# Loading w1 of a decode kernel by two transfers from two queues, with x behind the first

## The chip, the core and the metric

The kernel runs on one core of one Trainium2 chip. A core has TensorE (PE, with its weight loads shown apart as PEld), VectorE (DVE), ScalarE (ACT), GpSimd (POOL) and SyncE (SP); 16 DMA engines move data between the chip's main memory and the core's on-chip memory of 128 partitions. SyncE and ScalarE can both issue transfers, each on a queue of its own. The metric is the time of one execution in microseconds; shorter is better.

## What is computed

One decode step (one token for each of 4 batch rows, D = 576) of a block with two branches that share a layer norm of x: attention over the last 2048 positions of a cache of 16 KV heads with 32 query heads of 128, and a mixer followed by an MLP.

```python
x  = A_x                                   # [4, 1, 576]
xn = layernorm(x)
# branch A
q = xn @ wq                                # 32 heads of 128
k, v = the last 2048 rows of the caches    # 16 heads, each used by 2 query heads
A = softmax(q k^T / sqrt(128)) v @ wo
# branch B, on layernorm(xn)
h  = gelu(layernorm(xn) @ w1)              # 576 x 576
hs = shift(h) @ w2                         # shifts along the sequence, which has length 1
x1 = xn + hs
B  = x1 + gelu(layernorm(x1) @ w3) @ w4    # 576 x 4608, 4608 x 576
return x + A + B
```

With a sequence of length 1 every shift moves its rows out and zeros in, so the product with w2 is one with zeros.

## The kernel before, in words

Every engine's instructions are written out by hand: `add(engine, ..., key=...)` appends one with the events that it waits for and a sort key, and at the end each engine's list is sorted by key. `add_dma` does so for a transfer; each transfer counts on a semaphore of its own name, and the returned event is the full count of what has been issued under that name so far. Without `engine=` it goes to SyncE's list.

SyncE's list holds all the large transfers. By their keys: w1 (-50), w2 (-49), wq (-48), w3 (-47), then the 16 chunks of K (2 MB each, key 0 to 15), the 8 chunks of V (4 MB each, the last in two pieces), w4 and the five pieces of wo. The first four and the first two K chunks wait for nothing. K chunk 2 waits for the last matmul that reads wq (event "q"), as wq lies in the buffer of K's slots 2 and 3; from chunk 4 on, each waits until chunk c - 4 has been transposed. V and the last weights wait for buffers in the same way. A matrix of 576 rows is laid out by `runs`: 9 half rows lie one after the other on each of 128 partitions, so w1 and w2 are 128 rows of 5184 bytes each.

ScalarE's list begins with the transfer of x (4 rows of 1152 bytes, key -100) and ends with that of the output.

The work at the start, in order: VectorE takes the statistics of x (L305, L306, L308), ScalarE the square root (L310), VectorE normalises (L312, L314, L318), and does the same once more on xn for branch B. TensorE transposes both (L330), VectorE spreads them into `xs` (L336). TensorE then goes through its list in this order: the product with w1 (L397, nine matmuls, waits for w1 and xs), the two halves of the product with w2 (L405), the transposes of the third layer norm (L330), the product with wq (L369, 36 matmuls), transposes of q (L380), the zeroing of two PSUM banks (L360), and the product with w3 (L430), which waits for w3. After that comes the long part: for each K chunk 64 transposes (L485), copies out of PSUM on VectorE and ScalarE (L469, L468) and 16 score matmuls (L492); softmax; the products with V (L553); and the products with w4 and wo (L392), whose sum is copied to the output (L608, L609).

`t1`, the sum of x and x1 (L414), reads x once more and is used near the end.

Of the kernel before, what the change touches and what calls it, by code (L numbers as in the profile page):

```python
# [37 lines left out]
def bass_parallel_sum__sliding_block_cached__mixer_s_mlp__decode_kernel(  # L38
# [27 lines left out]
    x2 = A_x.rearrange("b s d -> (b s) d")  # L66
# [3 lines left out]
    with ExitStack() as ctx:  # L70
        def sb(name, shape, dt):
            return ctx.enter_context(nc.sbuf_tensor(name, shape, dt))

        def sem(name):
            return ctx.enter_context(nc.semaphore(name))
# [22 lines left out]
        def cut(n):  # L98
            nonlocal _o
            _o += n  # L100
            return ktb[:, _o - n:_o]
        w1_t = cut(9 * HALF)
# [10 lines left out]
        x_sb = sb("x_sb", [B, D], BF16)  # L113
# [74 lines left out]
        def add(engine, emit, waits=(), sig=None, key=0.0, inc=None):  # L188
            seqc[0] += 1
            prog[engine].append(Op(emit, waits, sig, key, seqc[0], inc))  # L190

        def add_dma(pairs, skey, waits=(), key=0.0, engine="sp"):
            if skey not in S:
                S[skey] = sem("s_" + "_".join(str(k) for k in (skey if isinstance(skey, tuple) else (skey,))))
            dma_count[skey] = dma_count.get(skey, 0) + 16 * len(pairs)

            def emit(e):
                for o_, i_ in pairs:
                    e.dma_start(o_, i_).then_inc(S[skey], 16)  # L199
            add(engine, emit, waits, None, key)  # L200
            return ("dma", skey, dma_count[skey])

        def runs(w_ap):
            return w_ap.rearrange("(m e) n -> m (e n)", e=9).rearrange("m (a x) -> (m a) x", a=2)
# [60 lines left out]
        add("dve", lambda e: e.tensor_copy(out=mH_bf[:], in_=mH[:].unsqueeze(2).to_broadcast([128, NX, 2])), waits=["mH"], sig="mH_bf", key=-7.8)  # L265


        ev_x = add_dma([(x_sb[:], x2)], "x", (), -100, engine="act")
        ev_wq = add_dma([(wq_t, runs(A_wq))], "wq", (), -48)
        ev_w1 = add_dma([(w1_t, runs(B_w1))], "w1", (), -50)  # L270
        ev_w2 = add_dma([(w2_t, runs(B_w2))], "w2", (), -49)
        ev_w3 = add_dma([(w3_t, runs(B_w3))], "w3", (), -47)
        ev_w4 = add_dma([(w4_t, B_w4.rearrange("(p r) n -> p r n", r=W4R))], "w4", [f"PV{2 * (NCV - NVS + 1) + 1}"], KS + NCV)
# [444 lines left out]
```

## Time and profile before

| | |
|---|---|
| median of 3 runs | 213.94 us (213.77 to 214.14) |
| the profiled execution | 213.93 us |
| its span in the profile | 212.6 us |
| PE / PEld busy | 172.5 us (81%) / 133.7 us (63%) |
| DVE / ACT / POOL busy | 111.9 us / 58.6 us / 15.6 us |
| DMA | 88.65 MB in 5066 packets, mean 417 GB/s |

The span is the stretch that the profiler records; the time of the execution is a little longer. In the lists of the trace, a row gives the source line (L199 is the line in `add_dma` that issues a transfer), the engine, the operation, the tiles written and read, and the count. "SPq" and "ACTq" are the instruction queues of SyncE and ScalarE, which issue transfers and count as busy with nothing else. In brackets stands how long the engine was idle before and what released it. "To landing" is the time from a transfer's issue to its completion. In a table of windows the columns are the stretch, its length, busy time (and instructions) of PE, PEld, DVE, ACT and POOL, the clock granted to TensorE, the mean busy share of the 16 DMA engines, and GB/s.

### The profile page before, as it was taken

To read this page: it belongs to the slowest core of one execution; us is meant where nothing else is said; L and a number is where in the kernel's file an instruction comes from. 1 tells how busy PE (TensorE), PEld (TensorE's weight loads), DVE (VectorE), ACT (ScalarE), POOL (GpSimd) and SP (SyncE) were. 2 spreads that over 40 slices of the span, in tenths; PEclk is the share of its full clock that TensorE was granted. 3 is DMA by queue.
4 is the path that set the end of the run, shared out by engine and by line. 5 is a ranking of instruction groups with operands and counts; after the bars stand their busy time and mean duration, and the time that the engine had idled before them with its cause. 6 is when DMAs were issued, how large, how long until landed. Compare 5 with 4: busy or idle time off the path is not lost.

```text
span 212.6 us, 4856 instructions
## 1 busy us (share of the span) xinstructions
PE 172.5 (81%) x2212; PEld 133.7 (63%) x2216; DVE 111.9 (53%) x168; ACT 58.6 (28%) x69; POOL 15.6 (7%) x38
## 2 busy tenths in 40 slices
PE   1456147999999999999996089999989598997495
PEld 0222014888878888887774048988868487883262
DVE  5433200477776777777764869995575444003000
ACT  2004001366665566666656520000000000000000
POOL 8991000000000000000000000000000000000000
PEclk9997855899999999999999589999999889999799
DMA  6999999999999999999999999999999999999993
GB/s 242 453 444 445 429 396 416 432 425 427 429 416 438 432 422 429 435 422 424 432 444 438 444 407 459 413 425 453 407 444 438 419 425 410 451 476 393 407 408 131
DMA packets 5066, 88.65 MB, mean 417 GB/s; under 512 B 568, under 2 KB 704, under 8 KB 1216
## 3 DMA queue, kind: packets, MB, share of 16 engines
q1 hardware_dynamic: 5040, 88.49, 97.7%
q8 instruction: 8, 0.13, 0.3%
q14 instruction: 2, 0.02, 0.0%
q10 hardware_dynamic: 16, 0.01, 0.0%
HBM read 88.49 MB, written 0.00 MB: 416 GB/s over the span
## 4 chain that ended last, share of the span: by engine, by line
DMA 47%; PE 45%; DVE 4%; SPq 1%; ACT 1%; issue 1%
PE ps L485 23%; DMA vring<-in_A_wo_dram 15%; DMA vring<-in_B_w_dram 13%; DMA vring<-in_A_v_cache_dram 12%; PE ps L553 11%; DMA kring<-in_A_k_cache_dram 7%; PE ps L492 6%; PE ps L430 2%; SPq L199 1%; DVE vring L520 1%; DVE rmax L498 1%; DVE ktb L545 1%; PE ps L514 1%; PE ps L347 1%; ACT ktb L468 0%
## 5 line engine op out<-in xcount | busy, mean ns | idle before, releaser
L469 DVE COPY ktb<-ps 128x1024 bf16<-128x1024 bf16 x80 | 53.8, 689 | 23.5 <-PE ps L485 23.4
L485 PEld LDWEIGHTS ps<-perm_bf,kring 128*128 128x128 bf16 x1024 | 58.2, 98 | 8.3 <-issue 7.6
L485 PE MATMUL ps<-perm_bf,kring 128*128 128x128 bf16 x1024 | 61.7, 220 | 0.2
L468 ACT ACTIVATE ktb<-ps 128x1024 bf16<-128x1024 bf16 x48 | 48.0, 1023 | 32.5 <-PE ps L485 32.1
L545 DVE TENSOR_TENSOR ktb<-kring,mH_bf 128x4096 bf16<-128x4096 bf16 x16 | 36.2, 2286 | 14.6 <-PE ps L553 14.6
L553 PE MATMUL ps<-vring,ktb 128*128 128x256 bf16 x256 | 30.3, 282 | 4.3 <-DMA vring<-in_A_v_cache_dram 3.5
L553 PEld LDWEIGHTS ps<-vring,ktb 128*128 128x128 bf16 x256 | 25.7, 101 | 8.5 <-issue 3.6
L553 PE MATMUL ps<-kring,ktb 128*128 128x256 bf16 x256 | 28.6, 273 | 0.9 <-DMA kring<-in_A_v_cache_dram 0.9
L553 PEld LDWEIGHTS ps<-kring,ktb 128*128 128x128 bf16 x256 | 25.0, 98 | 4.5 <-issue 1.1
L608 ACT ACTIVATE out_sb<-ps 4x288 bf16<-4x288 f32 x1 | 0.4, 399 | 84.6 <-PE ps L392 84.6
L492 PE MATMUL ps<-ktb,Qs 128*32 128x512 bf16 x272 | 17.8, 382 | 1.2 <-ACT ktb L468 1.2
L430 PE MATMUL ps<-vring,xs 128*8 128x320 bf16 (+1 forms) x72 | 4.5, 429 | 7.6 <-DMA vring<-in_B_w_dram 7.6
L492 PEld LDWEIGHTS ps<-ktb,Qs 128*32 128x32 bf16 x272 | 5.7, 96 | 6.7 <-DVE ktb L469 1.4
L514 PE MATMUL ps<-vring,pick_bf 128*32 128x256 bf16 x64 | 3.9, 411 | 6.4 <-DVE rinv L532 6.4
L609 DVE CAST out_sb<-ps 4x288 bf16<-4x288 f32 x1 | 0.4, 449 | 15.7 <-PE ps L392 15.7
L392 PE MATMUL ps<-vring,h2T_sb 128*4 128x288 bf16 x72 | 6.2, 347 | 3.1 <-DMA vring<-in_B_w_dram 3.1
L571 DVE TENSOR_SCALAR tmp<-ps,maskd 128x128 f32<-128x128 f32 x2 | 0.7, 350 | 14.8 <-PE ps L553 14.8
L430 PEld LDWEIGHTS ps<-vring,xs 128*8 128x8 bf16 x72 | 2.1, 110 | 9.8 <-DMA vring<-in_B_w_dram 8.0
L330 PE MATMUL ps<-ident_bf,xp_bf 4*128 4x4 bf16 x15 | 0.8, 163 | 8.1 <-DVE xp_bf L314 5.0
L392 PEld LDWEIGHTS ps<-vring,h2T_sb 128*4 128x4 bf16 x72 | 3.7, 101 | 5.8 <-DMA vring<-in_B_w_dram 3.6
L514 PEld LDWEIGHTS ps<-vring,pick_bf 128*32 128x32 bf16 x64 | 2.0, 118 | 8.2 <-DVE rinv L532 6.9
L239 POOL MEMSET ktb<- 128x8192 bf16 x1 | 6.9, 6924 | 0.0
(93 smaller groups left out, 78.6 us busy)
## 6 DMA issues: line engine op xcount, KB each, us to landing
kring<-in_A_k_cache_dram SPq DMA_DIRECT2D x16, 2048.0 KB, 13.8
vring<-in_A_v_cache_dram SPq DMA_DIRECT2D x4, 4096.0 KB, 24.6
kring<-in_A_v_cache_dram SPq DMA_DIRECT2D x3, 4096.0 KB, 34.0
vring<-in_B_w_dram SPq DMA_DIRECT2D x2, 5184.0 KB, 25.1
kring<-in_A_wq_dram SPq DMA_DIRECT2D x1, 4608.0 KB, 15.7
kring<-in_A_v_cache_dram SPq DMA_DIRECT2D x2, 2048.0 KB, 27.4
vring<-in_A_wo_dram SPq DMA_DIRECT2D x1, 1872.0 KB, 26.9
vring<-in_A_wo_dram SPq DMA_DIRECT2D x1, 1440.0 KB, 29.8
```

The source lines that it names most:

```text
L199: e.dma_start(o_, i_).then_inc(S[skey], 16)
L239: P(lambda e: e.memset(ktb[:, NKT // 2 * 1024:NKT * 1024], 0.0), key=-92, inc=(("E", LB - 2), 1))
L347: ins = e.matmul(ps[:, w, :], lhsT=zeros_bf[:, 0:128], rhs=zeros_bf[:, :], start=True, stop=True)
L392: return e.matmul(ACC[h], lhsT=lhsT, rhs=rhs, start=start, stop=stop, tile_position=(0, 32 * h), skip_group_check=True)
L430: ins = e.matmul(H2ps[k][32 * j:32 * j + 2 * B].rearrange("b (p t) -> b p t", t=n), lhsT=x_at(2, s_), rhs=w[:, :, 9 * j + t0:9 * j + t0 + ...
L468: return "act", lambda e: e.activation(out=ktbuf[:, n % NKT], in_=tb[n % 4], func=ACTF.Copy)
L469: return "dve", lambda e: e.tensor_copy(out=ktbuf[:, n % NKT], in_=tb[n % 4])
L485: ins = e.transpose(tb[j % 4][:, t, :], kslot_t(k)[:, 8 * kb + t, :], perm_bf[:])
L492: ins = e.matmul(Sps[32 * u:32 * u + 32, q, :].rearrange("p (t i) -> p t i", t=16), lhsT=Qs[:, k, 32 * u:32 * u + 32], rhs=ktgrp[:, (4 * k ...
L514: ins = e.matmul(ps[32 * j:32 * j + 32, 4 + qt, 256 * ih:256 * (ih + 1)].rearrange("p (t a e) -> p t a e", a=NPAIR, e=2), lhsT=pick_bf[:, ...
L545: return lambda e: e.tensor_tensor(out=PTpad[:, n % 4], in0=PTv[:, qt, NH * h:NH * (h + 1), bp, :].unsqueeze(2).to_broadcast([128, NH, NX, ...
L553: ins = e.matmul(ps[:, 0, 0:256], lhsT=PTpad[:, 2 * (k % 2) + h, 2 * g:2 * g + 2].rearrange("p t h e -> p (t h e)"), rhs=vslot(k)[:, Dh * ...
```

## The change

w1's single transfer from SyncE becomes two: the odd partitions are issued by ScalarE as the first entry of its list, in the place of x, and the even partitions by SyncE as the first entry of its list. Both count on the same semaphore, and the product with w1 waits for the full count of both. x is issued by SyncE with the key -49.5, that is between the even half of w1 and w2. Nothing else is changed.

```diff
-        ev_x = add_dma([(x_sb[:], x2)], "x", (), -100, engine="act")
+        ev_x = add_dma([(x_sb[:], x2)], "x", (), -49.5)
         ev_wq = add_dma([(wq_t, runs(A_wq))], "wq", (), -48)
-        ev_w1 = add_dma([(w1_t, runs(B_w1))], "w1", (), -50)
+        add_dma([(w1_t[1:128:2], runs(B_w1)[1:128:2])], "w1", (), -100, engine="act")
+        ev_w1 = add_dma([(w1_t[0:128:2], runs(B_w1)[0:128:2])], "w1", (), -50)
         ev_w2 = add_dma([(w2_t, runs(B_w2))], "w2", (), -49)
```

## The prediction

> **What bounds the kernel now.** I read the page's head first, then the DMA rate by stage, then the chain that ended last, then the first 30 us instruction by instruction.
>
> From the page: the span, the 40 slices of the span with the share and the rate of the DMA engines, and the one queue (SyncE's) that carries nearly all bytes.
>
> ```profile
> span 212.6 us, 4856 instructions
> ...
> DMA  6999999999999999999999999999999999999993
> GB/s 242 453 444 445 429 396 416 432 425 427 429 416 438 432 422 429 435 422 424 432 444 438 444 407 459 413 425 453 407 444 438 419 425 410 451 476 393 407 408 131
> ...
> q1 hardware_dynamic: 5040, 88.49, 97.7%
> q10 hardware_dynamic: 16, 0.01, 0.0%
> ```
>
> Only the first and the last slice are not full. The same by stages (the last two columns are the DMA share and GB/s):
>
> ```profile
> 0.00:2.50 2.50, 0.61 (x1) 0.10 (x1) 0.26 (x1) 1.10 (x1) 1.84 (x8) 1.00 0.26 60
> 2.50:30.00 27.50, 10.31 (x92) 4.99 (x96) 10.18 (x34) 3.07 (x7) 13.80 (x31) 0.85 1.01 429
> 30.00:110.00 80.00, 78.52 (x1309) 63.54 (x1303) 52.24 (x93) 45.58 (x47) 0.00 (x0) 0.94 1.01 430
> 110.00:176.00 66.00, 54.05 (x538) 44.59 (x537) 44.77 (x35) 8.47 (x15) 0.00 (x0) 0.92 1.00 428
> 176.00:208.50 32.50, 27.41 (x268) 19.82 (x268) 3.97 (x6) 0.00 (x0) 0.00 (x0) 0.95 1.00 424
> ```
>
> From 2.5 to 208.5 us the 16 DMA engines are full, at 424 to 430 GB/s, whatever the compute does. The kernel is a stream of 88.5 MB with a lead-in and a tail. The tail is short; from the chain that ended last (start, length, what):
>
> ```profile
> 2.17 27.46 DMA vring<-in_B_w_dram
> ...
> 178.35 31.68 DMA vring<-in_A_wo_dram
> 210.03 0.04 issue
> 210.07 0.70 PE ps L392 x8
> 210.78 0.44 DVE out_sb L609
> ```
>
> The last piece of wo is issued 31.68 us before it lands, so the queue is deep even at the end, and after that landing little more than 2 us follow. So the end moves by what the stream as a whole moves, one for one: it can start earlier or later, have a gap, or run at another rate. A delay of an engine counts only if it empties the queue, or if it outlasts the slack before a landing.
>
> **The change part by part.** The start of the timeline (start, length, engine, line, what, count, and in brackets the idle time before it and who ended it):
>
> ```profile
> 0.80 0.85 SPq L199 DMA_DIRECT2D ktb<-in_B_w_dram  x2
> 0.81 0.56 ACTq L199 DMA_DIRECT2D x_sb<-in_A_x_dram  x1
> ...
> 1.40 1.28 ACT L310 ACT_TABLE_LOAD   x1 [1.40 <-PEq L703]
> ...
> 2.17 0.52 SPq L199 DMA_DIRECT2D vring<-in_B_w_dram  x1
> 2.24 0.45 DVE L305 BATCH_NORM_STATS2 stats<-x_sb 4x6 f32<-4x288 bf16 x1 [2.24 <-DMA x_sb<-in_A_x_dram]
> ...
> 2.73 18.97 SPq L199 DMA_DIRECT2D kring<-in_A_k_cache_dram  x4
> ...
> 8.46 2.32 PE L397 MATMUL ps<-ktb,xs 128*8 128x288 bf16 x9 [0.78 <-DVE xs L336]
> ...
> 17.41 3.06 PE L369 MATMUL ps<-kring,xs 128*8 128x512 bf16 x36
> ...
> 21.57 0.54 PE L360 MATMUL ps<-zeros_bf 128*128 128x320 bf16 x2
> ...
> 29.68 2.57 PE L430 MATMUL ps<-vring,xs 128*8 128x320 bf16 x36 [7.56 <-DMA vring<-in_B_w_dram]
> ```
>
> And three answers on single transfers: the spread of the landing times of the B weights (w1 is the shortest, w3 the longest), the same for K, and one wait of SyncE's queue.
>
> ```profile
> DMA to landing us min/median/max: 3.6/13.9/27.5
> ```
> ```profile
> DMA to landing us min/median/max: 12.1/13.8/37.0
> ```
> ```profile
> SPq L199 <- PE ps L369: 16.5, 1, 16.5
> ```
>
> 1. *w1's two halves.* The bytes stay: two times 324 KB for one time 648 KB. I take it that all sixteen engines share each half; no row shows a transfer of 64 rows, and were each half on fewer engines, w2's bytes would fill the others. One transfer more has one more completion, which no row prices and which moves nothing. w1 lands 3.6 us after its issue, at 4.4 us. Its reader, the nine matmuls of L397, starts at 8.46 us, and what releases it is xs from VectorE, not w1. So w1 is 4 us early already. An earlier w1 is worth nothing by itself: its halves matter only through the stream's start.
>
> 2. *x.* It leaves ScalarE's queue, where nothing was ahead of it, and goes behind the even half on SyncE's. Bounds of its delay: at least its issue comes later by the issue of the half ahead (the two issues of w1 and w2 take 0.85 us together, so about 0.4 us each), that is +0.4 us; at most it lands with w1 as it lands today, at 4.4 instead of about 2.2 us, +2.2 us. The engines that carry x must first finish the even rows of their ring, with the odd rows coming in between, so I take +2.0 us. The whole layer norm chain behind x moves with it: L305 to L336 on VectorE and ScalarE, then PE in its order: L397, both L405, L369 (the q matmuls), the transposes, the zeroing of L360. That chain ends at 21.57 + 0.54 = 22.1 us and PE is then idle for 7.56 us, until w3 lands. So it ends at 24.1 us, with 5.6 us to spare. **Cost 0**; what hides it is the wait of L430 for w3, and the delay would have to exceed 7.56 us to show there. What is added in time by a lower TensorE clock if the q matmuls fall elsewhere is bounded by their own 3.06 us again, which still leaves 2.5 us.
>
> 3. *Who waits on that chain besides PE.* SyncE holds back K chunk 2 until the last q matmul (the wait of 16.5 us); it would be issued 2.0 us later, at about 22.5 us. The longest landing of a K transfer is 37.0 us; it belongs to one of the first two chunks, issued from 2.73 us on, so the queue has bytes until about 40 us. The issue comes 17 us before it is needed: **cost 0**, and the cover would be gone only at a delay of 17 us.
>
> 4. *SyncE's own issues.* x is one issue more on its queue (again about 0.4 us), the even half saves at most half of its 0.4 us. So w2 is issued between 0.2 and 0.6 us later than at 1.24, by 1.85 us at the latest, and wq, w3 and the first two K chunks move by as much. w2's bytes are wanted when w1's are through, by 4.4 us at the latest and not before 3.3 us (w1's 664 KB at the full rate take 1.55 us, from 1.7 us on). That w2's data follow its issue by 0.9 us (as w1's do: issue 0.80, first bytes at 1.7) gives 2.75 us. There is 0.5 us of cover at the worst: **cost 0**. ScalarE issues the odd half in place of x, 0.56 us today for four rows; its table load at 1.40 us could slip by the same, and is wanted only by the first Sqrt, after x.
>
> 5. *The stream's start, the only term left.* Windows of 0.1 us (the last column is GB/s):
>
> ```profile
> 1.60:1.70 0.10, 0.10 (x1) 0.00 (x0) 0.00 (x0) 0.10 (x1) 0.10 (x1) 1.00 0.00 0
> 1.70:1.80 0.10, 0.10 (x1) 0.00 (x0) 0.00 (x0) 0.10 (x1) 0.10 (x2) 1.00 0.18 46
> 1.80:1.90 0.10, 0.10 (x1) 0.00 (x0) 0.00 (x0) 0.10 (x1) 0.10 (x2) 1.00 2.24 311
> 1.90:2.00 0.10, 0.08 (x1) 0.00 (x0) 0.00 (x0) 0.10 (x1) 0.10 (x1) 1.00 1.26 259
> 2.00:2.10 0.10, 0.00 (x0) 0.00 (x0) 0.00 (x0) 0.10 (x1) 0.10 (x1) 1.00 0.71 156
> 2.10:2.20 0.10, 0.00 (x0) 0.00 (x0) 0.00 (x0) 0.10 (x1) 0.10 (x1) 1.00 0.22 52
> 2.20:2.30 0.10, 0.00 (x0) 0.00 (x0) 0.06 (x1) 0.10 (x1) 0.10 (x1) 1.00 0.44 156
> 2.30:2.40 0.10, 0.00 (x0) 0.00 (x0) 0.10 (x1) 0.10 (x1) 0.10 (x1) 1.00 0.68 259
> 2.40:2.50 0.10, 0.00 (x0) 0.00 (x0) 0.10 (x1) 0.10 (x1) 0.10 (x1) 1.00 0.69 259
> 2.50:2.60 0.10, 0.00 (x0) 0.00 (x0) 0.10 (x1) 0.10 (x1) 0.10 (x1) 1.00 1.23 467
> ```
>
> From 1.7 to 2.5 us the eight windows sum to 1498, so 150 KB came where 429 GB/s would have brought 343 KB. The missing 193 KB are 0.45 us of the stream. That is the **ramp**: w1's first packets, taken up at 1.8 us, are slow to finish. Bounds for the changed start: two queues fill the dip wholly, -0.45 us, and half as many rows on each queue come up to half an issue sooner, -0.19 us more; or the second queue goes through a ramp of its own that adds to the first, +0.45 us. In between: x on ScalarE's queue and w1 on SyncE's were issued at 0.81 and 0.80 us and the first bytes of both lie in the first two windows above, so ScalarE's queue starts no later. Half as many rows on each bring the rows forward by half of 0.19 us on average. I take **-0.1 us**, near the row of issues and not near an end, since the dip stands after the first bytes and no row says that a second queue fills it.
>
> The Trainium skill speaks against the change. Its page "DMA: Bandwidth & Descriptors", section "Rules for kernel authors", says of two transfers to disjoint partition halves that they are not worth it, since both spread over the same sixteen engines and serialize; one transfer is to be used. By that rule the ramp stays and the term is 0, not -0.1. The rows agree with it from 2.5 us on, where one queue runs at 429 GB/s; no row of this trace shows two queues in the dip.
>
> Sum: the profiled run took 213.93 us, of which 212.6 are the span, and the median of the three runs is 213.94, so the one stands for the other. 213.93 + 0 (w1) + 0 (x) + 0 (K's issue) + 0 (issues) - 0.1 (start) = **213.8 us**.
>
> **The rivals.**
>
> *Faster: the ramp goes.* Two rings on each engine, each with its first packet under way, fill the dip, and the stream's later landings all come sooner. For it: the dip is there, on every engine at once. Against it: an engine that is held up by its first packet may hold up both rings. Time: 213.93 - 0.45 = 213.5, with the earlier rows 213.3.
>
> *Slower: two ramps.* The odd rows' first packets are as slow as the even rows', one after the other on the same engine, and the stream starts later. Place: 1.7 to 3 us; price: 0.45 us, 214.4 us; if SyncE's added issue is then also exposed by 0.1 to 0.2 us ahead of w2, 214.5. It decides once w1's later half lands over 0.43 us after 4.4 us, and w3 with it. For it: the first packets are what is slow, and there will be twice as many first packets. Against it: at later boundaries between transfers (w1 to w2, w2 to wq) no dip is left in the stage's 429 GB/s.
>
> *The late x shows.* It would take a delay over 7.56 us at L430, and x would have to land after 9.8 us, behind w2 and part of wq. Ring order speaks against it. Price beyond that: little, as a late PE does not empty the queue. I fold it into the slower case.
>
> *The halves do not go at once.* If ScalarE's issue came late, the odd half would land later than the even one. L397 has 4 us of slack for that, the even half keeps the engines fed, and the time stays 213.9.
>
> **How the numbers follow.** A measurement of this kernel can tell about 0.2% (0.43 us) from no change, that is the band 213.5 to 214.4. The forecast with its neighbours (no gain in the dip at all, halves not at once) gets 0.50: its own range is 213.6 to 214.1. The filled ramp gets 0.27, since the gain needed to leave the band is nearly the whole of what the dip holds, but the earlier rows can add to it. Two ramps, with the exposed issue, get 0.23. The range takes in both ends and leaves out what goes beyond them: 213.3 to 214.5.
>
> **What would show it.** Right: the first-us windows bring their 150 KB or slightly more by 2.5 us, w3 lands and L430 starts at 29.6 to 29.7 us, L305 starts near 4.2 us, L397 near 10.5 us, PE's wait for w3 shrinks from 7.56 to about 5.6 us, and stages from 2.5 us on stay at 424 to 430 GB/s. The ramp rival: L430 at 29.2 us, and the last landing 0.4 us sooner. The two-ramps rival: L430 at 30.1 us. Wrong in its ground would be a stage rate that moves by over 1 GB/s (0.25% of the stream, 0.5 us), or a gap in the DMA share later on: then the stream isn't what I take it for.

## The result, and the profile after

The changed kernel takes 214.99 us (median; 214.86 to 215.20), the kernel before 213.93 us (213.77 to 214.14): a ratio of 1.0046, 95% interval 1.0035 to 1.0057, so it is **slower by 1.06 us**. Half a per cent is small, but it lies outside the range of the prediction. The profiled execution of the changed kernel took 214.87 us with a span of 213.6 us; lines from the change on are one higher than before (L398 is the product with w1, L431 that with w3).

The head of the page of the changed kernel, for the rows shown of before:

```profile
span 213.6 us, 4857 instructions
...
DMA  5999989999999999999999999999999999999992
GB/s 193 457 428 420 466 375 439 436 417 416 436 430 417 430 436 433 411 439 431 423 445 442 436 448 396 436 442 426 442 417 430 442 417 420 460 446 408 405 405 108
...
q1 hardware_dynamic: 4984, 88.17, 96.9%
q10 hardware_dynamic: 88, 0.34, 0.4%
```

The first slice brings 193 instead of 242 GB/s, the last 108 instead of 131. By stages (the last two columns are DMA share and GB/s):

```profile
0.00:2.50 2.50, 0.61 (x1) 0.10 (x1) 0.00 (x0) 1.09 (x1) 1.83 (x8) 1.00 0.17 29
2.50:30.00 27.50, 10.05 (x78) 4.67 (x78) 14.93 (x26) 2.48 (x6) 13.89 (x31) 0.94 1.00 422
30.00:110.00 80.00, 77.22 (x1305) 62.25 (x1299) 52.67 (x98) 45.92 (x47) 0.00 (x0) 1.00 1.01 430
110.00:176.00 66.00, 54.49 (x547) 44.98 (x546) 45.45 (x38) 9.39 (x16) 0.00 (x0) 0.90 1.00 428
```

From 30 to 176 us the rates are those of before, 430 and 428. What is missing is missing before 30 us: (60 - 29) x 2.5 + (429 - 422) x 27.5 = 270 KB, which at 429 GB/s are 0.63 us of the stream, averaged over the engines. The chain that ended last shows the same at two landings:

```profile
2.85 29.22 DMA vring<-in_B_w_dram
...
179.39 31.66 DMA vring<-in_A_wo_dram
211.05 0.04 issue
211.09 0.70 PE ps L393 x8
```

w3 lands at 32.07 us instead of 29.63 (2.44 later), the last piece of wo at 211.05 instead of 210.03 (1.02 later, which is the loss). A transfer has landed when its slowest engine is through, and the records of single DMA packets show how far apart the engines are: behind the data of each of these transfers stand 16 packets of 4 bytes, read here as one for each engine that is through. For w3 they lie between 28.70 and 29.26 us before the change; after it fifteen lie between 29.15 and 29.99 us and one at 31.66 us. So the 2.44 us are one engine's, the 0.63 us the mean. Where they arise is seen in the first microseconds. The timeline:

```profile
0.80 0.56 SPq L199 DMA_DIRECT2D ktb<-in_B_w_dram  x1
0.81 0.56 ACTq L199 DMA_DIRECT2D ktb<-in_B_w_dram  x1
...
1.42 0.51 SPq L199 DMA_DIRECT2D x_sb<-in_A_x_dram  x1
...
1.98 0.36 SPq L199 DMA_DIRECT2D ktb<-in_B_w_dram  x1
...
3.37 28.21 SPq L199 DMA_DIRECT2D kring<-in_A_k_cache_dram  x4
...
5.00 0.45 DVE L306 BATCH_NORM_STATS2 stats<-x_sb 4x6 f32<-4x288 bf16 x1 [5.00 <-DMA x_sb<-in_A_x_dram]
...
5.45 6.92 POOL L239 MEMSET ktb<- 128x8192 bf16 x1
...
6.49 6.18 DVE L315 TENSOR_SCALAR xn_bf<-x_sb,mv,rstd 4x576 bf16<-4x576 bf16 x1
...
16.97 2.32 PE L398 MATMUL ps<-ktb,xs 128*8 128x288 bf16 x9 [0.78 <-DVE xs L337]
...
26.87 3.48 PE L370 MATMUL ps<-kring,xs 128*8 128x512 bf16 x36
...
31.29 0.41 PE L361 MATMUL ps<-zeros_bf 128*128 128x320 bf16 x2
...
32.11 3.49 PE L431 MATMUL ps<-vring,xs 128*8 128x320 bf16 x72 [0.41 <-DMA vring<-in_B_w_dram]
```

Two things are to be seen. First, the issue of each half takes 0.56 us, and w2 leaves at 1.98 instead of 1.24 us. Second, x comes at 5.00 instead of 2.24 us, and the normalising instruction (L315), which took 0.42 us, now starts inside GpSimd's long memset and takes 6.18 us: it ends only when the memset is over. The product with w1 starts at 16.97 instead of 8.46 us. PE is ready for the product with w3 at 31.29 + 0.41 = 31.70 us, where it was ready at 22.11 us: 9.6 us later, and 2.07 us past the 29.63 us at which w3 landed before the change. That PE still waits 0.41 us for w3 is only because w3 comes later too.

The stream's start in windows of 0.1 us (last column GB/s):

```profile
2.00:2.10 0.10, 0.00 (x0) 0.00 (x0) 0.00 (x0) 0.10 (x1) 0.10 (x1) 1.00 0.00 0
2.10:2.20 0.10, 0.00 (x0) 0.00 (x0) 0.00 (x0) 0.10 (x1) 0.10 (x1) 1.00 2.29 311
2.20:2.30 0.10, 0.00 (x0) 0.00 (x0) 0.00 (x0) 0.10 (x1) 0.10 (x1) 1.00 1.35 259
2.30:2.40 0.10, 0.00 (x0) 0.00 (x0) 0.00 (x0) 0.10 (x1) 0.10 (x1) 1.00 0.37 104
2.40:2.50 0.10, 0.00 (x0) 0.00 (x0) 0.00 (x0) 0.10 (x1) 0.10 (x1) 1.00 0.32 52
```

The row with 311 stands at 2.1 us; before it stood at 1.8 us. The dip behind it is as deep as before. And the landings, from the issues by line (KB, us to landing), first those of the changed kernel, then those of the kernel before:

```profile
ktb<-in_B_w_dram SPq DMA_DIRECT2D x1, 648.0 KB, 6.9
...
ktb<-in_B_w_dram SPq DMA_DIRECT2D x1, 324.0 KB, 3.4
ktb<-in_B_w_dram ACTq DMA_DIRECT2D x1, 324.0 KB, 4.2
```
```profile
DMA to landing us min/median/max: 3.6/4.3/5.0
```

The halves land at 0.80 + 3.4 = 4.2 us and 0.81 + 4.2 = 5.0 us; w1 landed at 4.4. w2 lands at 1.98 + 6.9 = **8.9 us**, where it landed at 1.24 + 5.0 = 6.2. This landing of w2 is the number to follow in what comes.

The packet records say more. They do not name the engine, but on one engine each packet starts within some ns of the end of the one before, so chains can be put together. Most packets of w1 and w2 (5184 bytes) take 0.20 us. In the changed kernel the first even row starts at 2.15 us, the first odd row only at 3.33 us, which is when the first engine is through with its even rows (3.33 us). Then fifteen engines end w2 between 5.80 and 6.87 us, but one has a packet of w2 that takes 1.49 us (from 5.46 to 6.95) and ends w2 at 8.53 us. In the kernel before all engines end w2 between 5.33 and 5.92 us.

### The profile page after: what moved, and what is told of

Read it like the earlier page. It is cut to its first block, busy times and chain, and to the rows that moved or that the text cites. A ratio compares the mean times of both kernels' runs of the same rounds, so it can differ in the third digit from the quotient of the medians.

```text
span 213.6 us, 4857 instructions
## 1 busy us (share of the span) xinstructions
PE 172.4 (81%) x2212; PEld 133.3 (62%) x2216; DVE 117.9 (55%) x168; ACT 59.3 (28%) x69; POOL 15.7 (7%) x38
## 4 chain that ended last, share of the span: by engine, by line
DMA 61%; PE 31%; DVE 4%; SPq 2%; ACT 1%; issue 1%
DMA kring<-in_A_k_cache_dram 20%; DMA vring<-in_A_wo_dram 15%; DMA vring<-in_B_w_dram 14%; PE ps L486 12%; DMA vring<-in_A_v_cache_dram 12%; PE ps L554 11%; PE ps L493 4%; PE ps L431 2%; SPq L199 2%; DVE vring L521 1%; DVE rmax L499 1%; DVE ktb L546 1%; PE ps L515 1%; ACT ktb L469 0%; PE ps L348 0%
## 5 line engine op out<-in xcount | busy, mean ns | idle before, releaser
L486 PEld LDWEIGHTS ps<-perm_bf,kring 128*128 128x128 bf16 x1024 | 57.4, 98 | 9.3 <-issue 7.4
L469 ACT ACTIVATE ktb<-ps 128x1024 bf16<-128x1024 bf16 x48 | 48.6, 1024 | 31.6 <-PE ps L486 31.0
L331 PEld LDWEIGHTS ps<-ident_bf,xp_bf 4*128 4x128 bf16 x15 | 0.6, 102 | 17.5 <-POOL pick_bf L246 12.1
L311 ACT ACTIVATE sd<-mv 4x1 f32<-4x1 f32 x3 | 0.6, 203 | 22.1 <-DVE mv L309 22.1
```

The source lines that it names most:

```text
L469: return "act", lambda e: e.activation(out=ktbuf[:, n % NKT], in_=tb[n % 4], func=ACTF.Copy)
L486: ins = e.transpose(tb[j % 4][:, t, :], kslot_t(k)[:, 8 * kb + t, :], perm_bf[:])
```

## The experiments

Theory **S** (start) says that the loss is in the DMA stream's first microseconds: late first bytes and an engine that falls behind. Its rival **C** (chain) says that it is the late x: the layer norm held up by the memset, PE 8.5 us late. Later theories are named where they come up. The edits of 1, 4, 5, 14 and 15 are against the changed kernel, that of 9 against 3, the others against the kernel before; "..." in a line stands for what is left out of it. "Ratio" is against the kernel before on the same chip, with its 95% interval; "w2" is w2's landing in the profiled run, issue plus time to landing.

**1. x first on ScalarE's queue.** The odd half follows it there.

```diff
-        ev_x = add_dma([(x_sb[:], x2)], "x", (), -49.5)
+        ev_x = add_dma([(x_sb[:], x2)], "x", (), -100, engine="act")
-        add_dma([(w1_t[1:128:2], ...)], "w1", (), -100, engine="act")
+        add_dma([(w1_t[1:128:2], ...)], "w1", (), -99.5, engine="act")
```

> x goes back to the head of ScalarE's queue; the odd half follows it there, the even half stays on SyncE's. Theory S (start: two queues issuing large transfers side by side bring the first bytes later and leave one DMA engine behind, and the end moves with the stream): first bytes of w1 still late or slow, w3 lands over 1 us later than the 29.6 us of before, time 0.5 to 1.1 us over before (214.4 to 215.0). Theory C (chain: a late x puts the layer norm into GpSimd's long memset, VectorE's 0.42 us instruction takes 6.2 us, and the product with wq comes 9 us late): x at 2.2 us as before, the instruction 0.42 us again, PE's wait for w3 about 7.5 us, time as before, 213.9.

Measured: 214.55 us, ratio 1.0041 (1.0021 to 1.0062), single runs from 213.99 to 215.99. x came at 2.4 us and the chain was early, so C's 213.9 fails, though some executions were as quick as before. The profiled run was one of those (214.06 us), with w2 at 6.5 us. Five of the twelve took 215.18 us or more; none of these has a trace.

**2. x alone.** w1 whole, x behind it on SyncE's queue.

```diff
-        ev_x = add_dma([(x_sb[:], x2)], "x", (), -100, engine="act")
+        ev_x = add_dma([(x_sb[:], x2)], "x", (), -49.5)
```

> w1 stays whole on SyncE's queue, only x moves behind it. S: only one queue issues, first bytes at 1.8 us as before, w3 lands at 29.6 to 30.0 us, time 213.9 to 214.2. C: x lands near 4.5 to 5 us, the normalising instruction falls into the memset and takes about 6 us, time 214.9 to 215.0 as with the whole change.

```profile
1.65 0.35 SPq L199 DMA_DIRECT2D ktb<-in_B_w_dram  x1
```
```profile
DMA to landing us min/median/max: 3.7/5.2/6.8
```

Measured: 215.94 us, ratio 1.0087 (1.0074 to 1.0100): more than the whole change. Taken alone this spoke for C. But w2 landed at 8.4 us (1.65 + 6.8, both rounded) though only one queue issued, so S in its first form (two queues side by side) was wrong too. Here two engines were behind: they ended w2 at 7.17 and 8.11 us, the other fourteen by 6.11 us.

**3. The split alone on one queue.** Both halves on SyncE's queue, x on ScalarE's.

```diff
-        ev_w1 = add_dma([(w1_t, runs(B_w1))], "w1", (), -50)
+        add_dma([(w1_t[1:128:2], ...)], "w1", (), -50.5)
+        ev_w1 = add_dma([(w1_t[0:128:2], ...)], "w1", (), -50)
```

> Both halves on SyncE's queue one behind the other, x on ScalarE's as before. S: one queue, so no loss beyond one more issue, 213.9 to 214.2; if transfers of 64 rows at every second partition are slow by themselves, w1 lands well after 4.4 us and the time is 0.5 us or more over before. C: x early, 213.9.

```profile
0.80 1.81 SPq L199 DMA_DIRECT2D ktb<-in_B_w_dram  x3
```
```profile
DMA to landing us min/median/max: 3.3/3.8/6.8
```

Measured: 216.34 us, ratio 1.0109 (1.0094 to 1.0124), the worst so far, with x at 2.2 us and L315 at 0.42 us. C is not what costs here. w2, the third issue of the row above (from 2.04 us on), landed at 8.8 us. Four engines were behind: they ended w2 between 7.59 and 8.52 us, the other twelve by 6.59 us. The first bytes came at 2.13 us: the later start belongs to the half of alternate rows, not to the second queue.

**4. The whole change without the memset beside the layer norm.**

```diff
-        P(lambda e: e.memset(ktb[:, ...], 0.0), key=-92, inc=(("E", LB - 2), 1))
+        P(lambda e: e.memset(ktb[:, ...], 0.0), key=-80, inc=(("E", LB - 2), 1))
```

> The whole change, with GpSimd's memset of the upper half of ktb (6.9 us) put behind its other work, so that it no longer lies beside the first layer norm. S: VectorE's stall goes and the product with wq comes 6 us sooner, but w3's landing stays at 32 us and the time at 214.9 to 215.0. C: the time goes back to 213.9 to 214.2.

The normalising instruction, and the product with w3, in this kernel:

```profile
L315 DVE TENSOR_SCALAR xn_bf<-x_sb,mv,rstd x1: 434/434/434, 6.4 to 6.4; 4x576 bf16<-4x576 bf16 x1
```
```profile
31.32 4.29 PE L431 MATMUL ps<-vring,xs 128*8 128x320 bf16 x72 [6.62 <-DMA vring<-in_B_w_dram]
```

Measured: 215.16 us, ratio 1.0058 (1.0038 to 1.0077). The stall is gone (434 ns), PE again waits 6.62 us for w3, and nothing is gained. **C falls.** w2 landed at 8.1 us.

Now the kernels that lost in every run (2, 3 and the change) had seven transfers in SyncE's first burst; the kernel before had six, and so had 1, which lost in some runs. Theory **Q** took the number to be the cause.

**5. The whole change with K chunk 1 held back; 6. the same in the kernel before.** (`w` is what a K chunk waits for before it is issued; "hT" comes behind the product with w1.)

```diff
-            w = [...] if c >= N_CB else (["q"] if c >= 2 else [])
+            w = [...] if c >= N_CB else (["q"] if c >= 2 else ["hT"] if c == 1 else [])
```

> The whole change, with K chunk 1 issued only after the product with w1, so that SyncE issues six transfers in its first burst, as before the change, and not seven. Theory Q (burst: a seventh transfer in SyncE's first burst leaves one DMA engine about 2 us behind in w2's packets, and that engine ends last): w2's packets end together, w3 lands near 30 us, time 213.9 to 214.3, the rest being the later first bytes. Theory S (side-by-side issue from two queues): w3 lands at 32 us, time 214.9 to 215.2.

> The kernel before, with K chunk 1 issued only after the product with w1: five transfers in the burst. Q: no engine is behind, time 213.6 to 214.0. S: nothing is changed that matters, 213.9.

Measured: 214.81 us, ratio 1.0044 (1.0030 to 1.0059), with w2 at 7.2 us; and 214.00 us, ratio 1.0000 (0.9991 to 1.0008). Six in the burst did not bring the time back, and five did not better the kernel before. Both speak against Q.

**7. One transfer more at the end of the burst.**

```diff
+        x_more = sb("x_more", [B, D], BF16)
+        ev_xm = add_dma([(x_more[:], x2)], "xm", (), 1.5)
-            w = [...] if c >= N_CB else (["q"] if c >= 2 else [])
+            w = [...] if c >= N_CB else (["q"] + ([ev_xm] if c == 2 else []) if c >= 2 else [])
```

> The kernel before, with one more transfer of x (4 rows, into a tile that nothing reads) on SyncE's queue behind K chunk 1, the seventh of the burst. Nothing ahead of it moves. Q, if the number counts: an engine falls behind, 214.9 to 216. S, and Q if it is the place of x or of the half that counts and not the number: 213.9.

Measured: 216.80 us, ratio 1.0125 (1.0109 to 1.0142). It looks like a proof of Q and is none. The waits of SyncE's queue and a window of this kernel:

```profile
SPq L642 <- DMA x_more<-in_A_x_dram: 35.1, 1, 35.1
```
```profile
40.00:42.00 2.00, 2.00 (x39) 1.99 (x37) 1.80 (x4) 1.34 (x2) 0.00 (x0) 1.00 0.46 147
```

The small transfer lands in its turn, behind all that was issued ahead of it, at 39.7 us; K chunk 2 waited for it, and the stream ran dry (147 GB/s). The loss is the experiment's own wait.

**8. The burst spread out** in the kernel before:

```diff
-        ev_w3 = add_dma([(w3_t, runs(B_w3))], "w3", (), -47)
+        ev_w3 = add_dma([(w3_t, runs(B_w3))], "w3", ["ln1"], -47)
-            w = [...] if c >= N_CB else (["q"] if c >= 2 else [])
+            w = [...] if c >= N_CB else (["q"] if c >= 2 else ["hT"] if c == 1 else ["ln2"])
```

> The kernel before, with the burst spread out: w3 is issued after the first layer norm, K chunk 0 after the second, K chunk 1 after the product with w1, so three transfers stand in the burst. Q: the engines stay together, 213.4 to 213.9. S: 213.9, as all issues are still far ahead of their use.

Measured: 213.94 us, ratio 0.9999 (0.9990 to 1.0007). No gain.

**9. wq first.** As 3, but the long transfer goes ahead of the halves.

```diff
-        ev_wq = add_dma([(wq_t, runs(A_wq))], "wq", (), -48)
+        ev_wq = add_dma([(wq_t, runs(A_wq))], "wq", (), -51)
```

> Both halves of w1 on SyncE's queue and x on ScalarE's (as in the kernel that took 216.3), but wq, the long transfer of 11 us, goes first. w1, w2 and w3 are then issued with a long backlog ahead of them. Theory D (descriptors late: a transfer that is issued once the engines stream reaches one of them some us late, and costs that engine time if the backlog ahead of it is short): no engine runs dry, 213.9 to 214.4. Theory N (every further transfer ahead of w2 on SyncE's queue costs by itself): 216, as without the new order.

Measured: 214.19 us, ratio 1.0009 (1.0000 to 1.0018), against 1.0109 without the new order. The halves and w2 are the same transfers in the same sequence, with 13 us of wq ahead of them (w1's halves land 14.2 us after their issue): what comes late then is no loss; that the engines have other work meanwhile is the likely reason.

**10. w2 later, nothing added.**

```diff
-        ev_w2 = add_dma([(w2_t, runs(B_w2))], "w2", (), -49)
+        ev_w2 = add_dma([(w2_t, runs(B_w2))], "w2", [ev_x], -49)
```

> The kernel before, with SyncE waiting for x's landing (about 2.1 us) before it issues w2, so w2 and all behind it are issued about 1 us later. Same transfers, same queues, same order. D: w2's last packets come late on one engine, w3 lands 1 to 3 us later, time 214.9 to 216.5. N: nothing added, 213.9 to 214.1.

Measured: 214.16 us, ratio 1.0020 (1.0006 to 1.0033). w2 left at 2.58 us, later than with the change, and landed within 4.0 us, by 6.6 us. In the packet records nearly every engine has one slow packet of w2, most of 0.6 to 1.0 us, and none stays behind. So a late w2 costs something, but in this trace (214.25 us) it put no engine 2 us behind; D's 214.9 to 216.5 fails by the median. One of the twelve runs took 215.62 us and has no trace.

**11. x behind w2.**

```diff
-        ev_x = add_dma([(x_sb[:], x2)], "x", (), -100, engine="act")
+        ev_x = add_dma([(x_sb[:], x2)], "x", (), -48.5)
```

> w1 whole, w2 behind it at once as before, x behind w2 on SyncE's queue. x is late as with the change and VectorE's instruction falls into the memset. D: w2 is issued at 1.24 us as before, wq only 0.4 us later with 3 us of backlog, 213.9 to 214.5. N: w2 has nothing more ahead of it, 213.9. Theory X (the small transfer of x on SyncE's queue by itself puts an engine behind): 215 to 216.

```profile
2.99 1.27 SPq L199 DMA_DIRECT2D kring<-in_A_k_cache_dram  x2
```
```profile
7.78 5.63 DVE L314 TENSOR_SCALAR xn_bf<-x_sb,mv,rstd 4x576 bf16<-4x576 bf16 x1
...
32.44 3.50 PE L430 MATMUL ps<-vring,xs 128*8 128x320 bf16 x72
```

Measured: 213.99 us, ratio 1.0004 (0.9995 to 1.0013). x is even later than with the change, the instruction is held up for 5.63 us, PE reaches the product with w3 at 32.44 us without any wait left, 2.8 us later than before. **It costs nothing.** w2, issued at 1.24 us with only w1 ahead, landed at 6.3 us.

**12. The spare transfer of 7 without K chunk 2's wait for it.** SyncE waits for it at the very end; the line that makes `x_more` is as in 7.

```diff
+        ev_xm = add_dma([(x_more[:], x2)], "xm", (), 1.5)
         add("sp", lambda e: e.wait_ge(S[ev_o[1]], ev_o[2]), (), None, 10001)
+        add("sp", lambda e: e.wait_ge(S[ev_xm[1]], ev_xm[2]), (), None, 10002)
```

> The kernel before with the spare transfer of x behind K chunk 1, as in the run that took 216.8, but K chunk 2 does not wait for it (SyncE waits for it at the very end). D and N: 213.9, since the loss of that run came from K chunk 2, which waited for the spare transfer until 40 us and let the queue run dry. Theory Q (the number of transfers in the burst): 215 to 216.

Measured: 213.98 us, ratio 0.9999 (0.9990 to 1.0008). Seven transfers in the burst cost nothing; Q falls.

What is left is the place: theory **B** says that something short ahead of w2, behind w1 or its half, does it.

**13. x ahead of w1**, so that w2 is the third transfer, as in 2, and leaves at the same time.

```diff
-        ev_x = add_dma([(x_sb[:], x2)], "x", (), -100, engine="act")
+        ev_x = add_dma([(x_sb[:], x2)], "x", (), -50.5)
```

> w1 whole, no transfer from ScalarE's queue; x goes first on SyncE's queue, then w1, w2, wq. Everything is issued about 0.4 us later, and w2 is the third transfer of the queue. Theory T (whatever is third on the queue while the first bytes come reaches one engine late): w2's last packets late by 2 us on one engine, 215 to 216. Theory B (x or a half between w1 and w2 is what harms): no engine behind, only the 0.4 us, 214.1 to 214.5.

```profile
2.20:2.30 0.10, 0.00 (x0) 0.00 (x0) 0.06 (x1) 0.00 (x0) 0.10 (x1) 1.00 2.57 363
```
```profile
DMA to landing us min/median/max: 3.7/4.3/4.9
```

Measured: 214.37 us, ratio 1.0022 (1.0013 to 1.0031). w1's bytes start at 2.2 instead of 1.8 us, w2 lands at 1.64 + 4.9 = 6.5 us, no engine is behind, and the time is 0.43 us longer: a start that is 0.4 us later costs 0.4 us. The same transfers in the order of 2 cost 0.87%.

**14. The split, with x behind w2.**

```diff
-        ev_x = add_dma([(x_sb[:], x2)], "x", (), -49.5)
+        ev_x = add_dma([(x_sb[:], x2)], "x", (), -48.5)
```

> The split with both queues side by side as in the change, but x behind w2 on SyncE's queue. T: w2 is second, x third, no engine behind; what stays is the first bytes 0.35 us later and the slower ramp, 214.1 to 214.5. If the split by itself makes an engine fall behind: 215.

```profile
2.10:2.20 0.10, 0.00 (x0) 0.00 (x0) 0.00 (x0) 0.10 (x1) 0.10 (x1) 1.00 2.79 363
```
```profile
DMA to landing us min/median/max: 3.2/4.0/5.2
```

Measured: 214.41 us, ratio 1.0022 (1.0013 to 1.0031). Bytes start at 2.1 us, w2 lands at 1.42 + 5.2 = 6.6 us. This is the split's own price, 0.47 us.

**15. The change with wq ahead of w2.**

```diff
-        ev_wq = add_dma([(wq_t, runs(A_wq))], "wq", (), -48)
+        ev_wq = add_dma([(wq_t, runs(A_wq))], "wq", (), -49.2)
```

> The whole change, but wq (rows of 36 KB) is issued ahead of w2, so wq is third, behind the half of w1 and x. T: wq's first packets come late on one engine instead, with the same short backlog, 214.8 to 215.5. B with w2's short rows as the condition: 214.0 to 214.4.

Measured: 215.08 us, ratio 1.0054 (1.0041 to 1.0068). The split alone accounts for 214.41 us of this (14). In the packet records all 16 engines take up wq between 4.02 and 4.90 us, so none starts late; but one of the first packets takes 2.59 us, where the longest first packet of wq took 1.97 us in the kernel before. What stands behind x in that place loses time, whether its rows are of 5 or of 36 KB.

**16. The change again**, beside 13 to 15.

> The changed kernel unaltered, on the chip of the other three. All theories: 214.9 to 215.2, the last bytes of the stream about 1 us later than before.

Measured: 214.79 us, ratio 1.0038 (1.0025 to 1.0052); w2 at 1.98 + 5.6 = 7.6 us. Four engines end w2 between 6.58 and 7.25 us here, where one ended at 8.53 us before: how many engines lag, and by how much, differs from run to run.

**17. A spare transfer ahead of w2, all else as before; 18. the same bytes as 128 rows.** (In both, the wait at the end is as in 12, and in 17 `x_more` is as in 7.)

```diff
+        ev_xm = add_dma([(x_more[:], x2)], "xm", (), -49.5)
         ev_w2 = add_dma([(w2_t, runs(B_w2))], "w2", (), -49)
```
```diff
+        x_more = sb("x_more", [128, 18], BF16)
+        ev_xm = add_dma([(x_more[:], x2.rearrange("b (k x) -> (b k) x", k=32))], "xm", (), -49.5)
```

> The kernel before, x early on ScalarE's queue as it was; a spare transfer of x (4 rows of 1152 bytes, read by nothing) stands between w1 and w2 on SyncE's queue. Theory B (a small transfer between w1 and w2 is what puts an engine behind): 215 to 216, w3 lands 2 us late. If x must be late for it, or the second queue be idle: 213.9 to 214.2.

> The same, but the spare 4.5 KB come as 128 rows of 36 bytes, so that the engines share them evenly. If the four rows on few engines are what harms: 213.9 to 214.2. If any short transfer in that place harms: 215 to 216.

The issues and landings of 17, and the landings of 18:

```profile
1.24 0.36 SPq L200 DMA_DIRECT2D x_more<-in_A_x_dram  x1
1.65 0.35 SPq L200 DMA_DIRECT2D ktb<-in_B_w_dram  x1
...
2.99 2.25 SPq L200 DMA_DIRECT2D kring<-in_A_k_cache_dram  x2
```
```profile
DMA to landing us min/median/max: 3.5/5.2/7.0
```
```profile
DMA to landing us min/median/max: 3.6/4.7/5.9
```

Measured: 215.32 us, ratio 1.0056 (1.0035 to 1.0077), and 215.33 us, ratio 1.0065 (1.0053 to 1.0077). 4.5 KB that nothing reads, in front of w2, cost as much as the whole change, with x early and w1 whole. w2 lands at 1.65 + 7.0 = 8.7 us in 17 and at 1.70 + 5.9 = 7.6 us in 18, so four rows on few engines are not the point. In 17 two engines are behind (7.52 and 8.30 us, the other fourteen by 6.46 us); in 18 the ends are spread from 5.87 to 7.22 us. In 17 the two K issues take 2.25 us where 1.27 us are usual (11): SyncE itself is held up.

One rival is left untested: the moment instead of the place. In 2, 3, 17, 18 and the change, w2's issue begins 0.09 to 0.17 us before w1's first bytes move; in the kernel before and in 11 to 14 it begins 0.56 us or more before them. Only 10 moves w2's issue with nothing else, to 0.77 us after them, and it costs 0.2%. No run issued w2 at the critical moment with nothing between it and w1, so the two cannot be told apart here.

The runs in the order of w2's landing (15 has w2 behind wq, 7 and 9 are cases of their own). The landing is one profiled run's and that of its slowest engine alone, so it parts the dear versions from the cheap ones but does not rank the dear ones:

| kernel | w2 lands, us | ratio |
|---|---|---|
| before; 12; 11 | 6.2; 6.3; 6.3 | 1; 0.9999; 1.0004 |
| 13; 14; 10 | 6.5; 6.6; at most 6.6 | 1.0022; 1.0022; 1.0020 |
| 1 (profiled run one of its quick ones) | 6.5 | 1.0041 |
| 5; 16; 18 | 7.2; 7.6; 7.6 | 1.0044; 1.0038; 1.0065 |
| 4; 2; 17; 3; the change | 8.1; 8.4; 8.7; 8.8; 8.9 | 1.0058; 1.0087; 1.0056; 1.0109; 1.0046 |

No version beat the kernel before; 6, 8, 11 and 12 equal it.

## Why the prediction was wrong, point by point

**What bounds the kernel: right.** The time is the stream's: the rates from 30 to 176 us did not move, and the last landing came later by what the run lost (1.02 of 1.06 us). Experiment 13 bears out the rule "one for one": 0.4 us of start, 0.43 us of time.

**Part 1 (an earlier w1 is worth nothing): right.** The product with w1 is still released by xs, now at 16.97 us.

**Part 2 (x): the cost of 0 came true, but not for the reason given.** x came 2.76 us later, not 2.0. What the working missed is that the normalising instruction moves into GpSimd's memset: 6.18 instead of 0.42 us. PE was ready for w3 9.6 us later (31.70 instead of 22.11 us), more than the 7.56 us that were to hide it. So the condition of the rival "the late x shows" was met, and without x landing after 9.8 us. What held is that rival's price: "a late PE does not empty the queue". Experiments 4 and 11 show it: without the memset's delay nothing is gained, and in 11 PE comes 2.8 us later than before and the time stays. The Trainium skill, page "SBUF — State Buffer", section "Who interferes with whom", says that VectorE in a mode that uses two ports and GpSimd exclude each other from a shared pair of ports for a whole instruction, and that the one that issues first blocks the other. The trace agrees: 417 ns ahead of the memset, 6176 ns inside it, 434 ns with the memset moved away. That this instruction runs in such a mode no row shows.

**Part 3 (K chunk 2): right in its cost.** The last product with wq ended at 30.35 us (26.87 + 3.48), so chunk 2 left near 30 us and not at 22.5 us. That was still inside the cover, and the stage from 30 us on kept its 430 GB/s.

**Part 4 (SyncE's own issues cost 0): this step failed.** It took w2's data to follow its issue by 0.9 us, as w1's do on an idle machine, and found 0.5 us of cover. w2 left at 1.98 us, a little past the 1.85 us given as the latest (the issue of a half took 0.56 us, at most 0.4 was assumed), but it landed 2.7 us later. What the runs show in its place: with a further transfer on SyncE's queue between w1, or a half of it, and w2, one to four engines finish w2 0.5 to 2 us behind the others, or all are spread out (18), and the stream ends later. It was not seen with the transfer in another place (11, 12, 13) or with wq's long backlog ahead (9), and 4.5 KB are enough (17, 18). In the change this is what x does: the change costs 0.38 us more than the split with x behind w2 on the same chip (16 against 14), 0.58 us by the first six runs. Two things do not fit yet: some runs of 1 and one of 10 lost over 1 us with nothing in that place, and the moment of w2's issue was not parted from its place.

**Part 5 (the start, -0.1 us): failed in its sign.** The halves' first bytes come 0.3 us later, not 0.1 us earlier. A half of alternate rows takes 0.56 us to issue where the whole w1 took 0.37, and its first bytes come 1.33 us after the issue began (experiment 3, on one queue, as much) where the whole w1's came after 1.0 us. The term is +0.47 us (14). Half as many rows do not make half an issue.

**The rivals.** "Two ramps" gave 214.4 us, and the split alone gives 214.41; but the mechanism is a later start and not a second ramp, since the dip is as before. Its condition, that w1's later half lands over 0.43 us after 4.4 us, was met (5.0 us). "The halves do not go at once" came true in effect, though ScalarE's issue itself was not late (0.81 us): odd rows started 1.2 us behind the even ones. That this leaves the time at 213.9 was wrong. "Faster" did not happen. The rule of the Trainium skill, as the prediction told it, against two transfers to disjoint halves pointed the right way; by its reason, that they serialize, the price would have been 0, and the runs show 0.2%. The packet records agree with the reason: in the change, 16 and 14 the first odd row starts at 3.33, 3.31 and 3.23 us, and the first engine is through with its even rows at 3.33, 3.30 and 3.14 us.

**The range** ended at 214.5 because the exposed issue ahead of w2 was priced by its own length, 0.1 to 0.2 us. The price goes by the slowest engines of a transfer; in the change's trace one was 1.7 us behind the next at w2, the landing 2.7 us late, and 1.02 us of that were left at the end.

What stays open is why some engines are late. That their work orders (descriptors) reach them late would fit the held-up issue of K and the long packets of w2, but no row shows descriptors. Whether it is always the same engines was not shown either, as the records do not name them.

## What to carry to other kernels

In a kernel that is one long stream, the order of the first few transfers can be part of the critical path even when nothing waits for them. Here it paid to keep w1 and w2 whole and next to each other and the small transfer on the other queue or behind them. Look at the slowest landing of each transfer and not at the mean rate alone. An extra transfer that "only" costs an issue must be priced by what is behind it on the queue and by how much work the DMA engines have left at that moment. And if an instruction moves in time, look at what the other engines do where it lands.

## What the runs showed of the hardware that was not expected

- Issuing 64 alternate rows took 0.52 to 0.71 us; issuing the 128 rows of w1 as the first entry of the list took 0.37 us, those of w2 later in the list 0.33 to 0.72 us. The first bytes of w1 came 1.33 us after the issue of the half began, 1.0 us after that of the whole.
- Two queues that issue at the same moment did not start at the same moment: the odd rows on ScalarE's queue started at 3.33 us, the even ones on SyncE's at 2.15 us, and the odd ones began as the first engine was through with its even ones (3.33 us).
- A transfer of 4.5 KB between two of 648 KB cost 0.6% of a kernel of 214 us (1.0056 and 1.0065), with w2's landing 2.5 and 1.4 us late (8.7 and 7.6 instead of 6.2). The two profiled runs, 216.16 and 215.36 us, ended 2.2 and 1.4 us over the kernel before: little or nothing was made up in the 200 us that follow.
- VectorE's instruction of 0.42 us took 6.18 us beside GpSimd's memset of 6.9 us.
